# Chunks 0 and 1 of a delta-rule kernel rebuilt: four units side by side, 128-lane inversions, the pipeline from unit 4 on, and g @ w_out in step with the conversion of w_out

## The chip, the cores and the metric

The kernel runs on one core of a Trainium2 chip. The metric is the device time of one execution in microseconds (us). A profiled execution gives a span (first to last instruction) and a trace. The engines are PE (matrix multiplies; PEld is its weight load), DVE (vector), ACT (scalar), POOL (GpSimd) and SP, which issues most DMA transfers. Each engine works through its own instructions in order and meets the others by semaphores.

## The reference

Two stages. A delta rule runs over 768 positions for each of 4 x 8 heads with 48 columns, then a feed-forward block takes all 3072 rows:

```python
k_n = k / (np.linalg.norm(k, axis=-1, keepdims=True) + 1e-06)
for t in range(S):
    y[:, :, t] = np.einsum('bhd,bhde->bhe', q[:, :, t], state)
    v_old = np.einsum('bhde,bhd->bhe', state, kt)
    state = state + bt[:, :, :, None] * np.einsum('bhd,bhe->bhde', kt, vt - v_old)
# x = y as (3072, 384)
h = x @ w_in                              # 384 x 2048
g = h * (1.0 / (1.0 + np.exp(-1.702 * h)))
out = g @ w_out                           # 2048 x 384
```

The two weight matrices arrive in 64-bit floating point; the kernel converts them to 32 bits on the chip.

## The kernel before, in words

**Units.** The 768 positions are cut into 6 chunks of 128. A unit is one chunk c of one batch b with its 8 heads, `n = 4*c + b`, so there are 24 units; units 0 to 3 are chunk 0 and have no earlier state. Two units in a row make a pair, whose 256 rows go through the feed-forward block together.

**One unit.** `normalize` scales the keys. `prepare` transposes them (psT into kT), multiplies them with themselves (psG into G), and sends G through DRAM (Nd) so that the 32 x 32 blocks on its diagonal come back with one block a lane, in NT. A unit has 8 heads x 4 blocks = 32 blocks, so four units fill 128 lanes. `invert` (line 389) inverts these unit triangular blocks on DVE by row steps and then by products of halves, multiplies by beta into YS, and sends the result through DRAM (Yd) back as XB. It is a generator with 25 steps. For chunk 0 it runs once with 128 lanes; for each later pair of units once with 64 lanes. `Step.scores` (line 498) makes M, the masked product of keys and queries (psQ), with POOL's selection, and for c > 0 takes the state's share out of V. The substitution goes block by block: `solve` (psU, 16 records of PE, copied by ACT into US) and `below` (psR, subtracted from V by DVE in `rest`). `together` issues solves and belows of several units in turns. `outputs` multiplies M with US (psY) and copies the result to xT; `state` adds to ST. Some rows of xT go by six transfers from `last`.

**The feed-forward block.** `hidden` (line 623) computes ph = x @ w_in and ACT's Gelu into gT; `written` (line 644) computes po = g @ w_out and writes `out`. Both are generators that yield a cost in us. `take` draws from a queue of them.

**The weights.** `fetch` brings raw 64-bit parts into memory that w_out will fill later; `from_double` (line 166) converts a part with five operations on DVE, one of them followed by a Relu on ACT. w_in has 12 parts of 512 columns, w_out 16 of 384. A part can be fetched only when its place is free.

**The order.** Everything is issued from the end of the function (line 864 on): four units are prepared, `invert(0)` runs, three units are scored, and then step n runs for n = -1 to 24. A step works on three units at once: the last blocks of unit n-1 (A), the middle ones of n (B_) and the first of n+1 (D_). Steps up to 5 are `slot`, with six groups: each does some steps of the inversion, some parts of weights (WB = 1, 3, 5, 7, 8 per step) and feed-forward work for a share of 15.6 to 18.8 us; with nothing queued, `warm` runs small matmuls that only keep PE busy. Steps from 6 on are `woven`, with feed-forward work for 20.8 us in shares of a sixth. `pinned` (line 103) keeps an operation in the order in which it is written; a pinned operation is recorded in the trace at line 105, whatever its real line, so the groups are told apart by their tiles.

Of the kernel before, what the change touches and what calls it, by code (L numbers as in the profile page):

```python
# [18 lines left out]
def kernel(  # L19
# [33 lines left out]
    GR = 6  # L53
    NTH = HB * C
    FQ = 4
    GB = 4

    W0, W1, WB = 3, 1, (1, 3, 5, 7, 8)
    NA = W0

    NW, NA0, NY, NB0 = 80, 3, 48, 6
    XR = DP - D
    W = 6
    NS = C * C + C
    assert S % C == 0 and H == 8 and D <= DP and DM == H * D == KC * 128
    assert B == 4 and B * H * NB == 128 and FC == 4 * FQ
# [40 lines left out]
    in_order, now = [False], [0]  # L107

    class Engine:
# [5 lines left out]
        def __getattr__(self, name):  # L115
            op = getattr(self.engine, name)
            return pinned(op) if in_order[0] else op

    vec, act, pe = Engine(nc.vector), Engine(nc.scalar), Engine(nc.tensor)

    for i in range(B):
        nc.vector.memset(KN[i][:, :, D:DP], 0.0)
        load(i, ((KN, k),))

    bI = cpool.tile([128, NC, BS], F32, name="bI")
    betas = beta.rearrange("b h (c k j) -> (b h) c k j", k=NB, j=BS)
    for blk in range(NB):
        nc.scalar.dma_start(out=bI[blk::NB], in_=betas[:, :, blk, :])


    ident = cpool.tile([128, 128], F32, name="ident")
    make_identity(nc, ident)
    half = cpool.tile([128, H], F32, name="half")
    nc.gpsimd.memset(half, 0.5)

    nc.gpsimd.memset(YB, 0.0)
    nc.gpsimd.affine_select(
        out=YB, in_=YB, compare_op=ALU.not_equal, fill=1.0, base=0,
        pattern=[[1, BS], [-1, BS]], channel_multiplier=0,
    )  # L140


# [5 lines left out]
    def warm(n, after=None):  # L148

        ps = ps_moe.tile([128, 256], F32, tag="moe", name="ps_warm")  # L150
        if after is not None:
            after(ps[:, 0:1], 0.0)
        for _ in range(n):
            pe.matmul(ps, lhsT=ones[:, 0:128], rhs=ones, start=True, stop=True)  # L154

    warm(NW)
    table = cpool.tile([128, 1], F32, name="table")
    nc.scalar.activation(table, ident[:, 0:1], ACT.Copy)

    w_in = cpool.tile([128, KC, DFF], F32, name="w_in")  # L160
# [3 lines left out]
    nc.gpsimd.memset(low, -896.0 * (1 << 23))  # L164

    def from_double(dst, raw, n, alone):
# [5 lines left out]


        lo, hi = raw[:, :, 0], raw[:, :, 1]
        ts, stt = vec.tensor_scalar, vec.scalar_tensor_tensor
        if alone:
            ts, stt = pinned(ts), pinned(stt)
# [3 lines left out]

        ts(p, hi, 0x7FF * E1, None, op0=AND)
        if alone:
            ts(p, p, -896.0 * E1, 0.0, op0=ALU.add, op1=ALU.max)
            ts(p, p, 255.0 * E1, 8.0, op0=ALU.min, op1=ALU.mult)
        else:
            act.activation(p, p, ACT.Relu, scale=8.0, bias=low)
        yield
        t = wk.tile([128, n], I32, tag="P", name="tmp")
        f = t.bitcast(F32)  # L190
        ts(t, hi, E1 - 1, E1, op0=AND, op1=OR)
        stt(out=f, in0=lo.bitcast(U32), scalar=2.0**-32, in1=t, op0=ALU.mult, op1=ALU.add)
        stt(out=p, in0=hi, scalar=-(1 << 31), in1=p, op0=AND, op1=OR)
        stt(out=dst, in0=f, scalar=2.0**-20, in1=dst, op0=ALU.mult, op1=ALU.mult)
        yield

    N_IN = 512
    parts_in = KC * DFF // N_IN
    n_parts = parts_in + FC

    x_rows = [
        (ct * DP + o, (ct * NP + i) * D, m, step)
        for ct in range(2)
        for o, i, m, step in ((0, 0, D, D), (D, KC, XR, XR))
    ]

    stages, taken, made, begun = {}, {}, [], {}  # L210

    def stage(part):

        if part < parts_in:
            at = part % (2 * KC) * 2 * N_IN
            return at, at + 2 * N_IN
        f = part - parts_in
        if f >= FC - 2:
            return None
        depth = 2 if f < 2 or f >= 8 else 4  # L220
        if f >= 12:
            depth = 1
        at = FC * DM // (2 if f < 2 else 1) - (f % depth + 1) * 2 * DM
        return at, at + 2 * DM

    def together_with(part):

        return list(range(part, part + (KC if part < 3 * KC else 1)))

    def free(part):  # L230
        places = [s for p in together_with(part) if (s := stage(p)) is not None]
        return all(s[1] <= a or b <= s[0] for s in places for a, b in taken.values())

    def fetch(part, dma):

        if part < parts_in:
            j, f0 = part % KC, part // KC * N_IN
            parts = together_with(part)
            shape, src = (len(parts), N_IN), moe_w_in[:, f0 : f0 + N_IN]
            dst = w_in[:, j : j + len(parts), f0 : f0 + N_IN]  # L240
        else:
            parts = [part]
            shape, src = (1, DM), moe_w_out
            dst = target(part)
        if src.dtype != F32:
            if (s := stage(part)) is None:
                raw = wk.tile([128, *shape, 2], I32, tag="xT", name="raw", bufs=3)
            else:
                words = slice(s[0], stage(parts[-1])[1])
                raw = w_out.rearrange("p f d -> p (f d)")[:, words].bitcast(I32)  # L250
                raw = raw.rearrange("p (j n o) -> p j n o", j=shape[0], o=2)
            for i, p in enumerate(parts):
                stages[p] = raw[:, i]
                if s is not None:
                    taken[p] = stage(p)
            dst = raw.bitcast(src.dtype).rearrange("p j n o -> p j (n o)")
        if part < parts_in:
            for i in range(len(parts)):
                for p, r, m, step in x_rows:
                    dma(out=dst[p : p + m, i], in_=src[r + (j + i) * step : r + (j + i) * step + m])  # L260
        else:
            r = (part - parts_in) * 128
            dma(out=dst if src.dtype == F32 else dst[:, 0], in_=src[r : r + 128, :])
        return parts

    def target(part):
        if part < parts_in:
            j, f0 = part % KC, part // KC * N_IN
            return w_in[:, j, f0 : f0 + N_IN]
        return w_out[:, part - parts_in, :]  # L270

    def begin(part):

        if part not in begun:
            if part >= parts_in:
                a, b = (part - parts_in) * DM, (part - parts_in + 1) * DM
                if any(taken[p][0] < b and a < taken[p][1] for p in stages if p in taken):
                    return
            dst = target(part)
            begun[part] = from_double(dst, stages[part], dst.shape[-1], part < NA)  # L280
            next(begun[part])

    def convert(part):
        if part in stages:
            begin(part)
            if staged:
                begin(min(staged))
            stages.pop(part)
            next(begun.pop(part))

            made.append(part)
            while made and (len(made) > 1 or part < NA or part >= n_parts - 8):
                taken.pop(made.pop(0), None)


    ready = {}
    inverse = {}
# [431 lines left out]

    def slot(n, share):  # L730

# [197 lines left out]
```

## Time and profile before

| | us |
|---|---|
| median of three runs | 822.17 |
| all three | 822.04, 822.17, 824.47 |
| profiled execution | 821.86 |
| its span | 819.8 |
| PE busy in the span | 768.8 (94%) |
| DVE busy | 483.0 (59%) |
| ACT busy | 230.7 (28%) |
| POOL busy | 131.7 (16%) |
| mean granted clock of PE | 0.952 |

The profile's page cuts the span into 40 slices of 20.5 us; a digit is a busy share in tenths, and PEclk the clock granted to PE in tenths of full speed. A window line gives, for a stretch of the span, the busy time of each engine with its number of instructions. A timeline line gives start, duration, engine, line, operation, output<-inputs with shapes, and in brackets the idle time before and what ended it. In the trace each 32-bit matmul shows as two records; counts here are of records.

### The profile page before, as it was taken

The numbers are of one execution on the slowest core, as the hardware profiler recorded it, in microseconds if no ns is written. First come the engines' busy times: TensorE is split into PE (matmuls) and PEld (weight loads), VectorE is DVE, ScalarE is ACT, GpSimd is POOL, SyncE is SP. The second block draws the span as 40 slices with busy tenths as digits, with TensorE's granted clock in tenths as the row PEclk, the third lists the DMA queues.
The fourth block names the chain that finished last, engine by engine and source line by source line (L and its number), as shares of the span: only waits on it lengthen the run. The fifth ranks groups of instructions, "written<-read, shape, count | busy, mean of one in ns | idle before, by whom it ended". The sixth has DMA issues, their size and how long they took to land.

```text
span 819.8 us, 18780 instructions
## 1 busy us (share of the span) xinstructions
PE 768.8 (94%) x8100; PEld 577.4 (70%) x8100; DVE 483.0 (59%) x1037; ACT 230.7 (28%) x499; POOL 131.7 (16%) x138
## 2 busy tenths in 40 slices
PE   8429799889799999999999999999999999999998
PEld 7327688557676876867867867867768768677684
DVE  7797989787965675666667667666656730100000
ACT  2212543242232332322422322322322223212120
POOL 2013120322021222122123122212201000000000
PEclk9659889978979999999999999999999999999999
DMA  7986732721315123214204213213222020000000
GB/s 146 199 183 122 201 87 82 178 68 48 68 30 125 34 49 96 60 23 100 62 21 102 53 32 90 54 43 80 53 59 45 12 51 1 11 16 1 24 1 19
DMA packets 147698, 55.96 MB, mean 68 GB/s; under 512 B 114720, under 2 KB 143616, under 8 KB 147616
## 3 DMA queue, kind: packets, MB, share of 16 engines
q1 hardware_dynamic: 139872, 41.96, 24.0%
q0 software_dynamic: 2752, 10.62, 4.7%
q10 hardware_dynamic: 4992, 2.20, 1.0%
q8 instruction: 63, 1.03, 0.6%
q14 instruction: 19, 0.16, 0.1%
HBM read 33.13 MB, written 20.45 MB: 65 GB/s over the span
## 4 chain that ended last, share of the span: by engine, by line
PE 79%; DVE 6%; issue 6%; DMA 4%; SPq 2%; POOL 1%; ACT 1%; DVEq 0%; POOLq 0%; ACTq 0%
PE po L105 28%; PE ph L105 25%; PE psY L105 5%; PE psU L105 4%; PE psQ L105 3%; PE ps_warm L154 3%; PE ph L633 2%; PE psG L105 2%; PE psR L105 2%; DMA w_out<-in_moe_w_out_dram 2%; PE psT L105 1%; SPq L105 1%; DMA w_out<-in_moe_w_in_dram 1%; DVE tmp L105 1%; PE psG L362 1%
## 5 line engine op out<-in xcount | busy, mean ns | idle before, releaser
L105 PE MATMUL po<-w_out,gT 128*128 128x384 f32 x704 | 239.3, 490 | 0.0
L105 PE MATMUL ph<-xT,w_in 128*128 128x256 f32 x966 | 222.0, 384 | 0.3
L105 PEld LDWEIGHTS ph<-xT,w_in 128*128 128x128 f32 x966 | 180.3, 191 | 30.9 <-issue 2.3
L105 PEld LDWEIGHTS po<-w_out,gT 128*128 128x128 f32 x704 | 130.1, 190 | 82.6 <-issue 1.9
L105 DVE TENSOR_TENSOR V<-V,psR 64x384 f32<-64x384 f32 (+1 forms) x80 | 44.4, 556 | 194.8 <-PE psR L105 194.0
L105 DVE TENSOR_TENSOR P<-NT,YB 64x18 f32<-64x18 f32 (+25 forms) x171 | 82.3, 481 | 4.5
L105 ACT ACTIVATE gT<-ph 128x512 f32<-128x512 f32 x81 | 48.2, 595 | 115.9 <-PE ph L105 115.8
L105 DVE TENSOR_REDUCE YB<-P 64x6 f32<-64x18 f32 (+25 forms) x171 | 72.7, 425 | 5.5
L105 ACT COPY US<-psU 32x384 f32<-32x384 f32 x80 | 37.6, 470 | 131.9 <-PE psR L105 118.4
L528 POOL TENSOR_SCALAR_AFFINE_SELECT M<-M 128x1024 f32<-128x1024 f32 x24 | 29.8, 1240 | 226.6 <-DVE M L105 159.8
L105 PEld LDWEIGHTS psU<-V,XB 32*32 32x32 f32 x1280 | 45.9, 105 | 27.9 <-issue 20.5
L105 PE MATMUL psU<-V,XB 32*32 32x48 f32 x1280 | 54.3, 203 | 2.1 <-DVE V L105 2.1
L105 PE MATMUL psR<-US,G 32*32 32x48 f32 x1920 | 52.8, 203 | 0.0
L633 PE MATMUL ph<-xT,w_in 128*128 128x128 f32 (+1 forms) x282 | 47.0, 321 | 1.6 <-DMA xT<-last 1.6
L105 PEld LDWEIGHTS psR<-US,G 32*32 32x32 f32 x1920 | 44.6, 105 | 0.5 <-issue 0.5
L633 PEld LDWEIGHTS ph<-xT,w_in 128*128 128x128 f32 x282 | 40.3, 198 | 5.7 <-issue 2.4
L154 PE MATMUL ps_warm<-ident 128*128 128x256 bf16 x152 | 22.8, 318 | 16.7 <-DVE ps_warm L105 14.4
L90 POOL DMA_DIRECT2D KN<-in_k_dram x14 | 13.4, 955 | 153.1 <-PE psY L105 102.0
L308 POOL TENSOR_TENSOR rn<-ssq,half 128x8 f32<-128x8 f32 x17 | 36.9, 2169 | 2.9 <-DVE ssq L306 2.9
L105 ACT COPY o<-po 128x384 f32<-128x384 f32 x22 | 10.5, 479 | 77.7 <-PE po L105 55.8
L154 PEld LDWEIGHTS <-ident 128*128 128x128 bf16 x152 | 17.1, 114 | 21.0 <-issue 14.6
L105 DVE TENSOR_TENSOR P<-NT 64x256 f32<-64x256 f32 (+7 forms) x36 | 30.3, 841 | 0.3
(144 smaller groups left out, 871.0 us busy)
## 6 DMA issues: line engine op xcount, KB each, us to landing
Nd<-G SPq DMA_DIRECT2D x20, 512.0 KB, 3.5
w_out<-in_moe_w_out_dram POOLq DMA_DIRECT2D x14, 384.0 KB, 3.7
QP<-in_q_dram SPq DMA_DIRECT2D x24, 192.0 KB, 3.9
V<-in_v_dram SPq DMA_DIRECT2D x24, 192.0 KB, 3.0
out_dram<-o SPq DMA_DIRECT2D x24, 192.0 KB, 1.9
w_out<-in_moe_w_in_dram SPq DMA_DIRECT2D x18, 192.0 KB, 5.2
NT<-Nd SPq DMA_DIRECT2D x24, 128.0 KB, 2.6
Yd<-YS SPq DMA_DIRECT2D x24, 128.0 KB, 2.5
```

What stands on the lines that cost most here:

```text
L90: dma(out=dst[n % len(dst)][:, :, 0:D], in_=src[b, :, c * C : (c + 1) * C, :].rearrange("h p d -> p h d"),)
L105: return lambda *a, **kw: tc.keep_in_program_order(op(*a, **kw))
L154: pe.matmul(ps, lhsT=ones[:, 0:128], rhs=ones, start=True, stop=True)
L308: nc.gpsimd.tensor_tensor(rn, ssq, half, op=ALU.pow)
L362: pe.matmul(ps[h % 2][:, h // 2], lhsT=kT[r, h // 2, :], rhs=kT[r, h // 2, :], start=True, stop=True,)
L528: nc.gpsimd.affine_select(out=self.M, in_=self.M, compare_op=ALU.is_gt, fill=0.0, base=0, pattern=[[0, H], [1, 128]], channel_multiplier=-1,)
L633: pe.matmul(ph[:, u], lhsT=w_in[:, j, f * 128 : (f + 1) * 128], rhs=xT[:, j, t], start=(j == 0), stop=(j == KC - 1),)
```

## The change

Nothing changes in what is computed. In the new code:

- Keys of units 0 to 3 are normalized in one go, with the squares on ACT. A product of the transposed keys is made early (`turn`, `diagonal`), and only the 32 x 32 blocks are copied out and sent through DRAM as rows; the whole G of these units is made later (`gram`), while DVE inverts.
- All units 0 to 3 are scored before the substitution. Their POOL selections (`select`) wait on a `gate` that reads YS.
- The substitution of chunk 0 runs as units 0 and 1 side by side, then units 2 and 3 (`hops`), each ended by `put_out`.
- Units 4 to 7 are normalized and prepared during the second of these (`keys`), and inverted together with 128 lanes (`invert(1)`), beside the rest of `hidden` of pairs 0 and 1.
- Weights are converted in one sequence (`conversions`): w_in in 8 pieces of 3 x 256 columns, then w_out in 12 single and 2 double rows. `fill(n)` issues the next n operations of it. Each finished piece can trigger a fetch; all fetches go by SP, except half of the first two quarters of w_in, which go by POOL.
- `both_written` makes po of units 0 and 1 together and issues, ahead of each row f, as much of the conversion as that row needs and three operations more.
- `slot` is gone. `woven` runs from n = 3, with a share of 10.4 for n = 3 to 6 and 20.8 after.
- gT has 8 buffers instead of 4; some of them (`spare`) hold other tiles early. All vector, scalar and tensor operations are pinned now, as were those before step 2 and from step 6 on.

The core of the diff:

```diff
-    NW, NA0, NY, NB0 = 80, 3, 48, 6
+    GB = 8
     XR = DP - D
-    W = 6
+    NW, NA, NY, NU = 80, 3, 28, 4
+    NQ = DFF // 4
+    NPC = DFF // 8
     NS = C * C + C
...
+    def conversions():
+        whole = list(pieces())
+        def begin(i):
+            dst, raw, shape, name = whole[i]
+            ops = conversion(dst, places[name[1]] if raw is None else raw, shape)
+            next(ops)
+            return ops
+        after = begin(0)
+        yield
+        for i in range(len(whole)):
+            ops = after
+            next(ops)
+            yield
+            next(ops)
+            yield
+            if i + 1 < len(whole):
+                after = begin(i + 1)
+                yield
+            next(ops)
+            yield
+            next(ops)
+            done.add(whole[i][3])
+            fetches.pop(whole[i][3], lambda: None)()
+            yield
...
+    fetches = {
+        ("in", 1): lambda: fetch_in(2),
+        ("in", 3): lambda: fetch_in(3),
+        ("in", 5): lambda: fetch_out(3),
+        ("in", 7): lambda: (fetch_out(4), fetch_out(5), fetch_out(6), fetch_out(7)),
+        ("out", 4): lambda: fetch_out(13),
+        ("out", 6): lambda: fetch_out(12),
+    }
+    for new, old in ((8, 0), (9, 1), (10, 2), (11, 8), (14, 9), (15, 10)):
+        fetches[("out", old)] = lambda f=new: fetch_out(f)
+    converting = conversions()
+    def fill(n):
+        for _ in range(n):
+            next(converting, None)
...
+    def normalize_mixed(n):
+        K = KN[n % len(KN)][:, :, 0:D]
+        ksq = wk.tile([128, H, D], F32, tag="ksq", name="ksq", bufs=1)
+        act.activation(ksq, K, ACT.Square)
+        yield
+        ssq = wk.tile([128, H], F32, tag="ssq", name="ssq", bufs=4)
+        vec.tensor_reduce(ssq, ksq, axis=AX.X, op=ALU.add)
+        rn = wk.tile([128, H], F32, tag="rn", name="rn", bufs=4)
+        pool.tensor_tensor(rn, ssq, half, op=ALU.pow)
+        yield
+        vec.tensor_scalar(rn, rn, 1e-6, None, op0=ALU.add)
+        vec.reciprocal(rn, rn)
+        vec.tensor_tensor(K, K, rn.broadcast_to([128, H, D]), op=ALU.mult)
+        yield
...
+        for b in range(B):
+            act.activation(sq[:, b % 2], KN[b][:, :, 0:D], ACT.Square)
+            vec.tensor_reduce(s[:, b], sq[:, b % 2], axis=AX.X, op=add)
...
+        ready[n] = KN[n % len(KN)], kT, G
+        return G
...
+    def turn(n):
+        kTs[n] = wk.tile([128, NP, 128], F32, tag="kT", name="kT", bufs=6)
+        transposed(KN[n % len(KN)], kTs[n])
+    def prepare(n):
+        c, b = units[n]
+        turn(n)
+        yield 0.6
+        G = gram(n)
         Nd = dram.tile([H * NS], F32, tag="Nd", name="Nd", bufs=4)
-        dma = pinned(nc.scalar.dma_start) if c == 0 else nc.sync.dma_start
+        dma = sync if c < 3 else nc.sync.dma_start
...
+        dma(
...
+    def diagonal(b, D_):
+        kT = kTs[b]
+        ps = [ps_seq.tile([128, NP, 128], F32, tag="seq", name="psD") for _ in range(2)]
+        for h in range(H):
+            r = slice(h % 2 * 64, h % 2 * 64 + D)
+            pe.matmul(
+                ps[h % 2][:, h // 2], lhsT=kT[r, h // 2, :], rhs=kT[r, h // 2, :],
+                start=True, stop=True,
+            )
+        for e in range(2):
+            for blk in range(NB):
+                u = slice(blk * BS, (blk + 1) * BS)
+                copy = vec.tensor_copy if e == 0 or blk == 0 else act.copy
+                copy(D_[u, e::2, :], ps[e][u, :, u])
...
         YS = wk.tile([128, BS, BS], F32, tag="P", name="YS")[part]
         vec.tensor_tensor(YS, Y, bc, op=ALU.mult)
...
+        if c == 0:
+            gate = wk.tile([128, 1], F32, tag="gate", name="gate", bufs=1)
+            pool.tensor_copy(gate, YS[:, 0, 0:1])
+        dma = sync if c < 3 else nc.sync.dma_start
+        groups = [range(b0, b0 + nb)] if c > 0 else [range(HB), range(HB, B)]
+        back = {}
+        for bs in groups:
+            for b in bs:
+                back[b] = dram.tile([H * C, BS], F32, tag="Yd", name="Yd", bufs=4)
+                (beside if c == 0 and b >= HB else dma)(
+                    out=back[b].rearrange("(p j) i -> p j i", j=BS),
+                    in_=YS[(b - b0) * NB * H : (b - b0 + 1) * NB * H],
+                )
+            for b in bs:
+                XB = wk.tile([128, H, BS], F32, tag="XB", name="XB", bufs=4)
+                dma(out=XB, in_=back[b].rearrange("(h t) i -> t h i", h=H))
+                inverse[c * B + b] = XB
         yield 0.0
...
+        def select(self):
+            (pool if self.n < B else nc.gpsimd).affine_select(
...
+    def both_written(c, gT):
+        po = [ps_moe.tile([128, DM], F32, tag="moe", name="po") for _ in range(HB)]
+        for n, f in enumerate(order):
+            while ("out", f - f % 2 if 4 <= f < 8 else f) not in done:
+                fill(1)
+            fill(3)
+            for i in range(HB):
+                pe.matmul(
+                    po[i], lhsT=gT[f // FQ][:, f % FQ, i * C : (i + 1) * C], rhs=w_out[:, f, :],
+                    start=(n == 0), stop=(n == FC - 1),
+                )
+            if n < FC - 1:
...
-    def slot(n, share):
...
-                warm(NB0)
-        if n + 1 == len(WB) - 1:
-            run(weights(n_parts))
-        if n == W - 1:
-            next(new_step(n + 2).scored, None)
-        if n % HB == 0:
-            run(inverting)
-        follow(n)
...
+        if n % HB == 0 and n > B:
             h = (n - 1) // HB
-            if h == 0:
-                i = (n - 1) % HB
-                queue.append(hidden(xTs[h], gT0, slice(i * C, (i + 1) * C), 0.67))
-            if n % HB == 0:
-                gT = gT0 if h == 0 else []
-                if h > 0:
-                    queue.append(hidden(xTs[h], gT, slice(0, NTH), 1.3))
-                queue.append(written(*units[h * HB], gT))
-                xTs.pop(h)
+            gT = []
+            queue.append(hidden(xTs[h], gT, slice(0, NTH), 1.3))
+            queue.append(written(*units[h * HB], gT))
+            xTs.pop(h)
...
-        debt[0] += cost
+        debt[0] = debt[0] + cost if queue else 0.0
...
-        m, late = n + B + 1, n == W
+        m = n + B + 1
         K = normalize(m) if m < len(units) else iter(())
         P = prepare(m) if m < len(units) else iter(())
-        Q = prepare(m - 1) if late else iter(())
-        if n % HB == 1 and n + 1 + HB < len(units):
+        if n % HB == 1 and B < n and n + 1 + HB < len(units):
             inverting = invert(*units[n + 1 + HB], HB)
-        ahead = [8] * 3 if late else STEPS[:3] if n % HB == 1 else STEPS[3:]
+        ahead = STEPS[:3] if n % HB == 1 else STEPS[3:]
...
-        spend(share / 6)
-        next(Q, None)
-        spend(share / 6)
+        spend(share / 3)
...
+        sync(out=bI[blk::NB, 0], in_=betas[:, 0, blk, :])
...
+    fetch_in(0, other_queue)
...
+    warm(NW)
+    normalize_first()
+    Ds = spare("blocks").rearrange("p (b h j) -> p b h j", b=B, j=BS)
+    Nds = []
+    turn(0)
+    for b in range(B):
+        if b + 1 < B:
+            turn(b + 1)
+        diagonal(b, Ds[:, b])
+        Nd = dram.tile([H * C * BS], F32, tag="Nd", name="Nd", bufs=4)
+        sync(out=Nd.rearrange("(h p k) -> p h k", p=C, k=BS), in_=Ds[:, b])
+        Nds.append(Nd)
+    for b in range(B):
+        sync(
+            out=NT[b * NB * H : (b + 1) * NB * H].rearrange("d i k -> d (i k)"),
+            in_=Nds[b].rearrange("(d r) -> d r", r=BS * BS),
+        )
...
+    fetch_in(1, other_queue)
...
+    fill(6)
+    for b in range(B):
+        gram(b)
+        warm(NA)
+    pair = [new_step(n) for n in range(B)]
+    inverting = invert(0)
+    for n in range(B):
+        next(pair[n].scored)
+        warm(NA)
+        run(pair[n].scored)
+        warm(NA)
+        if n == 0:
+            ahead_of(inverting, 18)
+    run(inverting)
+    for s in pair:
+        s.select()
+    fill(5)
+    def hops(a, b):
+        yield [(a, 0)], []
+        for blk in range(NB - 1):
+            yield [(b, blk)], [(a, blk)]
+            yield [(a, blk + 1)], [(b, blk)]
+        yield [(b, NB - 1)], []
+    def put_out(s):
+        s.queries()
+        s.outputs(True)
+        steps.pop(s.n)
+    def keys():
+        def unit(n):
+            yield from normalize_mixed(n)
+            yield from prepare(n)
+        work = [unit(n) for n in range(B, 2 * B)]
+        for t in range(18):
+            for u in range(B):
+                s = t - 3 * u
+                if s >= 0 and s % 2 == 0:
+                    next(work[u], None)
+            yield
+        for w in work:
+            run(w)
+    path = hops(*pair[:2])
+    for i in range(2 * NB):
+        together(*next(path))
+        warm(NU)
+        fill(1)
+    for s in pair[:2]:
+        put_out(s)
+        fill(1)
+    load(7, ((KN, k),), sync)
+    load(8, ((KN, k),), sync)
+    for f in range(3):
+        fetch_out(f)
+    for n in range(B, B + 2):
+        load(n, ((QP, q),), sync)
+    ffn = []
+    def feed(n=1):
+        for _ in range(n):
+            while ffn and next(ffn[0], None) is None:
+                ffn.pop(0)
+    gTs = [], []
+    ffn.append(hidden(xTs[0], gTs[0], slice(0, NTH), 1.3))
+    path = hops(*pair[2:])
+    preparing = keys()
+    for i in range(2 * NB):
+        together(*next(path))
+        if i > 2:
+            feed()
+        fill(2)
+        ahead_of(preparing, 2 if i else 0)
+    for s in pair[2:]:
+        put_out(s)
+        feed()
+        fill(2)
+        ahead_of(preparing, 2)
+    ffn.append(hidden(xTs[1], gTs[1], slice(0, NTH), 1.3))
+    xTs.pop(0), xTs.pop(1)
+    load(B + 2, ((QP, q),), sync)
+    for n in range(B, B + 2):
+        load_values(n, sync)
+    while not ("in", 7) in done:
+        fill(1)
+    run(preparing)
+    inverting = invert(1)
+    first = new_step(B)
+    for i in range(25):
+        ahead_of(inverting, 1)
+        feed()
+        if i == 16:
+            next(first.scored)
+        if i == 18:
+            run(first.scored)
+    run(inverting)
+    while ffn:
+        feed()
+    fill(10)
+    queue = [both_written(0, gTs[0]), written(*units[HB], gTs[1])]
+    for n in range(B - 1, len(units) + 1):
+        woven(n, 20.8 if n > 6 else 10.4)
```

## The prediction

> **What bounds the kernel now.** I read the slices first, then the stretches of the span by engine, then single rows. The slices:
>
> ```profile
> PE   8429799889799999999999999999999999999998
> DVE  7797989787965675666667667666656730100000
> PEclk9659889978979999999999999999999999999999
> ```
>
> From slice 12 on (about 254 us) PE is full at full clock; before that DVE is the fuller engine and the clock dips. The same in four stretches (columns: length, then busy us of PE, weight load, DVE, ACT, POOL, then granted clock, DMA share, GB/s):
>
> ```profile
> 0.00:67.40 67.40, 38.44 (x298) 30.95 (x298) 57.26 (x140) 15.67 (x32) 13.10 (x32) 0.72 0.96 177
> 67.40:232.00 164.60, 146.20 (x1856) 113.58 (x1856) 138.01 (x305) 60.59 (x130) 32.31 (x39) 0.89 0.42 101
> 232.00:254.45 22.45, 22.45 (x260) 15.75 (x260) 20.05 (x33) 6.45 (x14) 4.41 (x4) 0.90 0.23 57
> 254.45:820.00 565.55, 561.68 (x5694) 417.13 (x5692) 267.65 (x562) 148.03 (x324) 81.87 (x64) 1.00 0.19 46
> ```
>
> 67.4 us is the first substitution (psU), 254.45 the end of unit 5's outputs (psY). After it PE bounds; before it DVE does 158 us of work in 187 us. So the change acts on the time until unit 5's outputs, and what follows it is counted in PE records. The waits of the first part, from the timeline (start, duration, instruction, idle before):
>
> ```profile
> 31.00 1.22 DVE L105 TENSOR_TENSOR NT<-NT,bI 128x1024 f32<-128x1024 f32 x1 [3.11 <-DMA NT<-Nd]
> ...
> 57.88 1.23 DVE L456 TENSOR_TENSOR YS<-YB,bI 128x1024 f32<-128x1024 f32 x1
> ...
> 67.44 0.86 PE L105 MATMUL psU<-V,XB 32*32 32x48 f32 x16
> ```
>
> The first inversion waits for its blocks until 31.0; YS ends it; the first solve follows 8 us later, behind 48 + 18 warm-up matmuls.
>
> **The tail, by records.** At the end PE runs one pair's ph (96 records) and po (64) back to back:
>
> ```profile
> 775.08 20.72 PE ph L105 x96
> 795.80 20.66 PE po L105 x64
> ```
>
> So a pair costs 41.38 us, a po record 0.323, a ph record 0.216. Before, 669 po and 960 ph records start after 254.45: 216.0 + 207.2 = 423.2 us. After the change, steps 3 to 6 spend 10.4 each on pairs 0 and 1 (41.6 in all, just their po: 41.3); at unit 5's outputs four of step 6's six shares are spent, so 3.5 is left, and ten pairs: 413.8 + 3.5 = 417.3. The attention work after that point is the same code. The rest is 565.4 (254.45 to 819.8) - 5.9 = **559.5 us**.
>
> **First solve: 67.4 to 60.** Squares go to ACT and one chain of small operations normalizes four units instead of two chains; but PE's 80 warm-ups end at 13.9 either way, so that earns nothing. Then PE needs 0.44 (psT x4) + 1.09 (psG x16) a unit; block copies cost DVE 5 x 0.28 a unit (row: last<-psY on DVE, 281 ns) and ACT 3 x 0.27 + 0.6, each within 1.53. Last copy 13.9 + 0.6 + 4 x 1.53 + 1.6 = 22.2. SP carries four beta loads more (one sixth of 24 KB each; before, all beta went by ACT) and six of the first quarter's twelve (0.42 each; POOL's six 0.54, ahead of memsets that nothing early needs): over by 10 us, before the blocks. Writing the blocks (a 128 KB transfer lands in 2.6 to 3.3) and reading them as whole rows (Yd: 2.2) gives NT at 28.0 instead of 31.0. The six conversion steps before it (4.6 us) lie in that wait, as 10 us of conversion did. The inversion took 26.9; two conversion operations in it (0.33 and 0.61 net) and two slow products beside POOL's selection (0.7, 0.2) are taken out: 25.0. YS ends at 54.2. The added gate holds POOL's four selections (1.1 to 1.3 each) behind YS: done by 60, first needed at 74. Yd to XB issue took 2.0, landing 3.3: 59.5; 28 warm-ups at 0.158 end before. First solve 60. Bounds: 57 if small blocks land as fast as Yd, 64 if as slowly as the 5.0 of the last G write.
>
> **Pairs 0/1: 60 to 78.5.** Eight calls: PE 0.88 (16 psU and 48 psR), then DVE 0.56, or 1.12 for block 0, plus 0.2 of signalling: 1.2 + 2 x 2.2 + 4 x 1.65 + 1.3 = 13.5; one more for Relu (some 1.0 on ACT) ahead of a US copy; two put_outs at 2.0. Warm-ups (4 x 0.145) and one conversion operation lie in the gaps. Before, the staggered start took 67.4 to 102 for two units.
>
> **Pairs 2/3: 78.5 to 112.** A conversion piece of 768 columns I scale from the rows of 384 and 512 columns (0.35, 0.42 and 0.55, 0.69): 2 x 0.56 + 3 x 0.97 = 4.0. A call has DVE 0.75 + 2 x 0.84 + 0.6 (norms of units 4 to 7: 4 x 1.47 spread) = 3.05, PE 0.88 + 1.3 + 0.7 = 2.9. So 2.2 + 2 x 2.9 + 5 x 3.05 + two put_outs at 3.3 = 30. **An added wait:** w_in's last quarter is asked for at 79.5, behind six xT transfers on SP (0.58 each) and needs 12 issues (0.42) and 5.1 to land: 92, wanted at 88.5. V's subtractions, norms and through V the next solves queue behind it on DVE: 3.5. Bounds 0 to 10 (issues of up to 1.5 are in the row).
>
> ACT's Square now alternates with the Gelu; the trace shows one table load of 1.28 at the first Gelu, and none for Relu and Copy after it, but has no Square. Up to two more loads, 0 to 2.6 us, on ACT, which is busy 2.3 of 3.05 a call: I take 0. The Trainium skill, "ScalarE: Activation LUTs", section "Table sets: the hidden batching unit", names relu, copy, identity and abs as in every set, not square, and its budget of about 2.7 us a switch would make it 5.3; an estimate that speaks against the change, and no run here shows it.
>
> **Inversion 1: 112 to 156.5.** One inversion of 128 lanes replaces two of 64 lanes: a product over 1024 columns is 1.22 in both, so 26 us of DVE go. It waits for unit 7: G copies 1.2, SP behind four w_out fetches, G's write 3.6, NT 2.6: starts 122; 25 + 1 (psQ subtractions) + 1.5 (their wait for PE) + 1.2 = 150.7. Beside it PE's 25 feeds take 32.4 + 2: to 147, so PE hides little more than DVE's wait. Ten conversion steps (5.5) follow, while XB lands: 156.5. Bounds 150 to 162.
>
> **Steps 3 and 4: 156.5 to 196.5.** By the order written out, 27 and 32 conversion operations at 0.47 (2.35 a piece: 0.35, 0.35 and 3 x 0.55), with subtractions, sums and norms 2 and 4: 18 + 19; PE's share is 13.3 and 16. Two gaps of 0.9, where three operations run ahead cover 1.4 of PE's 2.3; 1 for a fetch: 40. The nearest rows say the same: before, 14 conversions with two units' substitutions filled 144 to 182:
>
> ```profile
> 160.00:170.00 10.00, 9.25 (x52) 4.67 (x45) 8.97 (x20) 3.16 (x7) 5.08 (x6) 0.83 0.31 71
> 170.00:180.00 10.00, 7.62 (x99) 5.25 (x100) 8.07 (x24) 5.21 (x11) 3.40 (x3) 0.75 0.18 52
> 180.00:190.00 10.00, 10.00 (x103) 6.08 (x100) 5.76 (x15) 1.18 (x4) 0.97 (x1) 0.56 0.37 93
> ```
>
> These rows also show the clock falling to 0.56 where PE waits piecewise. For the whole start I add 4 (bounds 0 and 10). By the Trainium skill, "TensorE: Matmul & The Clock Gate", Part 1, "What's actually happening", the clock halves only after an idle window of about 3.4 us; no gap in my steps is that long, so by the rule the 4 is 0 and the end 798. The row differs: waits of under 2 us on PE lie in this stretch.
>
> **Step 5 and step 6 to unit 5's outputs: 40.** PE 10.4 + 8.5 (29.15 a step less 20.7) = 18.9, DVE 17 to 18 in line with it by sections: 21.5; NT of unit 9 comes 2.5 late; step 6 to the end of psY 16.
>
> **Sum.** 60 + 18.5 + 33.5 + 44.5 + 40 + 40 + 4 = 240.5, + 559.5 = 800.0 span; the profiled run took 821.86 for a span of 819.8, so 802.1; its time lies 0.3 under the median of 822.17.
>
> **Rivals.**
> - *DVE stays as full as it was* (0.845 until 254.45). My DVE work from first solve to that point is 135 (conversions 60, inversions 48, the rest 27): 160 us, unit 5's outputs at 220, end 781.5. For it: idle waits were short; against: NT of unit 7 and the feeds leave 10 us that nothing fills. Chance 0.12.
> - *The transfers come late*: quarter 3 at its 10, inversion 1 at 162, 4 more in step 5's NT and fetches: 6.5 + 5.5 + 4 = 16, end 818. The DMA share of 0.96 at the start speaks for it, 0.42 later against. 0.10.
> - *Slower: DVE and PE take turns in steps 3 and 4.* If three operations ahead cover nothing, PE's 29.3, less the 2.8 of gaps that I count already, stand behind DVE's 37: +26, 828. It decides once unit 5's outputs end 20 us after my 240.5. For it: po before waited for w_out (3.5 on weight loads) at low clock; against: those waits were 0.5 to 1.7 each. 0.16.
> - *It does not do what it says:* DVE only shifts the same waits, outputs at 256 to 261: 817.5 to 823, no change. 0.07.
>
> **Chances.** My case (786 to 814) 0.55. A measurement here tells about 0.3%, 2.5 us. Faster 0.55 + 0.12 + 0.10 = 0.77, same 0.07, slower 0.16. The range reaches to the first rival's time and leaves out what lies beyond it and most of the third: 781 to 824.
>
> **What would show it.** First solve by 60; NT at 28; DVE inverting at 122, idle ahead of it; one inversion of 128 lanes; psY of unit 5 ending near 240; then steps of 29.2 at full clock. Wrong if the clock in steps 3 to 6 is near 0.6, if conversions wait on transfers for over 10 us, or if steps from 7 on are not PE's.

## The result, and the profile after

Median after the change 823.73 us (20 runs, 818.19 to 831.47), before 824.63 (20 runs, 819.54 to 828.87): ratio 0.9989, interval 0.9965 to 1.0012. No change that can be measured. The forecast was 802.1. The profiled run took 823.91 for a span of 822.2 us.

The slices of the kernel after (tenths of each fortieth of the span):

```profile
PE   8678699777789999999999999999999999999998
DVE  5896671897679656675666566567665650110000
PEclk9686669889899999999999999999999999999999
```

PE is full from the thirteenth slice on, as it was before. DVE is no longer the fuller engine ahead of that; neither engine is full throughout. The chain of waits shows the last pair at the end of the run:

```profile
777.27 20.72 PE ph L102 x96
797.99 20.65 PE po L102 x64
```

That tail is the forecast's to 0.1 us a pair. So whatever was forecast and did not come is missing earlier. The stretches, cut where DVE starts or ends the stage (columns as before: length, busy us of PE, weight load, DVE, ACT, POOL, then granted clock, DMA share, GB/s):

```profile
0.00:61.90 61.90, 44.76 (x385) 35.22 (x386) 48.51 (x106) 23.80 (x54) 16.46 (x39) 0.81 0.81 135
61.90:84.60 22.70, 19.86 (x412) 15.65 (x413) 14.44 (x21) 6.69 (x14) 0.55 (x1) 0.70 0.38 81
84.60:128.00 43.40, 35.21 (x479) 27.64 (x477) 27.01 (x46) 18.80 (x36) 9.11 (x7) 0.69 0.63 137
128.00:146.15 18.15, 18.15 (x96) 15.73 (x95) 1.82 (x3) 5.21 (x10) 0.80 (x1) 1.00 0.62 164
146.15:174.10 27.95, 21.12 (x97) 17.67 (x96) 26.47 (x53) 6.54 (x14) 1.09 (x1) 0.88 0.21 38
174.10:228.00 53.90, 41.96 (x351) 24.85 (x353) 40.95 (x85) 17.56 (x33) 8.64 (x7) 0.84 0.43 111
228.00:263.00 35.00, 31.92 (x512) 21.52 (x507) 30.97 (x69) 10.82 (x27) 10.60 (x8) 1.00 0.24 60
263.00:822.00 559.00, 555.29 (x5672) 414.16 (x5672) 271.20 (x562) 148.67 (x325) 80.43 (x64) 1.00 0.20 47
```

The rows are: to the first solve, pairs 0/1, pairs 2/3, the wait for the second inversion's blocks, that inversion, conversions with steps 3 and 4, the rest to unit 5's outputs, the tail. In the fourth row DVE works 1.82 us of 18.15. The rows of DVE that mark the stages, from the timeline (start, duration, instruction, idle before it):

```profile
29.92 1.23 DVE L102 TENSOR_TENSOR NT<-NT,bI 128x1024 f32<-128x1024 f32 x1 [2.01 <-DMA QP<-in_q_dram]
...
55.18 1.23 DVE L102 TENSOR_TENSOR YS<-YB,bI 128x1024 f32<-128x1024 f32 x1
...
101.21 0.69 DVE L102 TENSOR_SCALAR w_in<-w_out 128x768 int32<-128x768 int32 x1 [6.14 <-DMA w_out<-in_moe_w_in_dram]
...
146.15 1.22 DVE L102 TENSOR_TENSOR NT<-NT,bI 128x1024 f32<-128x1024 f32 x1 [16.29 <-DMA NT<-Nd]
...
172.91 1.22 DVE L102 TENSOR_TENSOR YS<-YB,bI 128x1024 f32<-128x1024 f32 x1
```

Two waits for transfers stand out: 6.14 us for w_in's last quarter (the w_out buffer holds its raw form) and 16.29 for the blocks. SP's queue shows what the transfers were behind (start, time that the issues took, how many):

```profile
85.01 4.27 SPq L102 DMA_DIRECT2D xT<-last  x6
89.38 5.68 SPq L102 DMA_DIRECT2D w_out<-in_moe_w_in_dram  x12
...
130.14 3.68 SPq L102 DMA_DIRECT2D xT<-last  x6
133.87 2.00 SPq L102 DMA_DIRECT2D w_out<-in_moe_w_out_dram  x4
135.97 0.38 SPq L102 DMA_DIRECT2D Nd<-G  x1
143.58 0.32 SPq L102 DMA_DIRECT2D NT<-Nd  x1
```

Both times six xT transfers go first. The last unit's G is written only after them and after four fetches of w_out, and that write takes 7.6 us where the three before it took 3.2 to 4.3 (from the issue at 111.41, 119.14 and 125.92 to the issue of the read behind each). The waits of DVE and of PE from 173 to 262 us (total, times, longest):

```profile
DVE V L102 <- PE psR L102: 10.1, 4, 4.0
DVE V L102 <- PE psQ L102: 2.5, 4, 1.9
```

```profile
PE po L102 <- DVE w_out L102: 9.6, 5, 2.9
PE po L102 <- ACT w_out L102: 4.3, 1, 4.3
```

Here each waits for the other: DVE 12.6 us for PE, PE 13.9 us for a converted row of w_out.

### The profile page after: what moved, and what is told of

It is laid out like the page before. It is cut to its first block, busy times and chain, and to the rows that moved or that the text cites. A ratio compares the mean times of both kernels' runs of the same rounds, so it can differ in the third digit from the quotient of the medians.

```text
span 822.2 us, 18456 instructions
## 1 busy us (share of the span) xinstructions
PE 768.3 (93%) x7984; PEld 572.4 (70%) x7984; DVE 461.4 (56%) x939; ACT 238.1 (29%) x513; POOL 127.7 (16%) x126
## 3 DMA queue, kind: packets, MB, share of 16 engines
q8 instruction: 63, 1.03, 0.5%
## 4 chain that ended last, share of the span: by engine, by line
PE 76%; DVE 14%; DMA 4%; SPq 2%; ACT 1%; issue 1%; POOL 0%; DVEq 0%; POOLq 0%; ACTq 0%
PE po L102 29%; PE ph L102 26%; PE psY L102 6%; PE psU L102 5%; DVE P L102 4%; PE psQ L102 3%; DVE YB L102 3%; PE psG L102 3%; PE psT L102 2%; DMA w_out<-in_moe_w_in_dram 2%; PE psR L102 2%; SPq L102 2%; DVE NT L102 1%; DVE w_out L102 1%; DVE tmp L102 1%
## 5 line engine op out<-in xcount | busy, mean ns | idle before, releaser
L102 PE MATMUL po<-w_out,gT 128*128 128x384 f32 x768 | 271.3, 502 | 14.0 <-DVE w_out L102 9.6
L102 PE MATMUL ph<-xT,w_in 128*128 128x256 f32 x1152 | 268.1, 390 | 0.3
L102 PEld LDWEIGHTS ph<-xT,w_in 128*128 128x128 f32 x1152 | 218.7, 193 | 34.4 <-issue 1.5
L102 ACT ACTIVATE gT<-ph 128x512 f32<-128x512 f32 x96 | 56.4, 595 | 140.6 <-PE ph L102 140.5
L102 DVE TENSOR_TENSOR P<-NT,YB 64x8 f32<-64x8 f32 (+31 forms) x190 | 88.9, 468 | 5.4
L102 PEld LDWEIGHTS psU<-V,XB 32*32 32x32 f32 x1536 | 62.3, 110 | 40.7 <-issue 28.0
L102 DVE TENSOR_REDUCE YB<-P 64x4 f32<-64x8 f32 (+31 forms) x190 | 81.0, 426 | 6.5
L102 PE MATMUL psU<-V,XB 32*32 32x48 f32 x1536 | 73.6, 210 | 5.9 <-DVE V L102 5.2
L102 PE MATMUL psQ<-QS,kT 48*128 48x176 f32 (+1 forms) x384 | 35.9, 329 | 6.1 <-ACT QS L102 6.1
L102 PE MATMUL ps_warm<-ident 128*128 128x256 bf16 x176 | 29.9, 327 | 12.5 <-ACT G L102 7.4
L294 POOL TENSOR_TENSOR rn<-ssq,half 128x8 f32<-128x8 f32 x16 | 36.5, 2279 | 12.6 <-DVE ssq L102 12.6
L102 PEld LDWEIGHTS psQ<-QS,kT 48*128 48x128 f32 x384 | 29.6, 198 | 9.1 <-ACT QS L102 7.9
L102 DVE TENSOR_REDUCE NT<-P 64x64 f32<-64x1024 f32 (+7 forms) x40 | 32.6, 815 | 1.4
L102 PE MATMUL psG<-kT 48*128 48x128 f32 x384 | 32.0, 313 | 0.2
```

Of the source, the lines that this page charges most:

```text
L102: return lambda *a, **kw: tc.keep_in_program_order(op(*a, **kw))
L294: nc.gpsimd.tensor_tensor(rn, ssq, half, op=ALU.pow)
```

## The experiments

Five causes were put up. (1) The clock: pairs 0 to 3 ran at 0.69 to 0.70, and more warm-up matmuls would mend it. (2) The last quarter of w_in comes late, behind the xT transfers. (3) The last unit's blocks come late, through their place in the order and through the four fetches beside them. (4) DVE's conversions stand on the path in steps 3 and 4, and ten of them would have been free in the wait ahead of the inversion. (5) Three operations of look-ahead are too few. Against all five stands the rival that these waits cover one another, so that taking one away only brings up the next.

All ratios are to the kernel before, which ran beside each experiment. The kernel after did not: a gain "against the change" sets two such ratios against each other, and part of it can be another chip or another clock. Stage times are the starts of DVE's rows: ST of units 1, 3 and 5 (each unit's outputs), NT and YS of the second inversion. For the kernel after they are 84.2, 127.6, 263.0, 146.15 and 172.9.

### The clock: e1_more_warm and e2_no_warm

```
e1: hops of units 0/1:  warm(NU) -> warm(10)
    hops of units 2/3: + warm(30 if i == 3 else 6)   ahead of fill(2)
e2: hops of units 0/1: - warm(NU)
```

> The changed kernel with more warm-up matmuls in the substitution of chunk 0: 10 instead of 4 a call for units 0 and 1, and 6 a call (30 in the call where the weights come late) for units 2 and 3. Theory A, the granted clock (0.70 and 0.69 in these two stretches, where I had priced 4 us for the whole start) makes them long: the clock rises above 0.85, the stretch from the first solve to the last psY of unit 3 falls from 66.6 us to 55 to 59, the time by 7 to 10 us against the changed kernel. Theory B, the stretch is a chain of DVE, ACT and PE that wait for each other in turn, whatever the clock: the clock rises and the stretch stays at 66 or grows by what the added matmuls take (up to 8 us).

> The changed kernel without the four warm-up matmuls a call for units 0 and 1. Theory A: the clock there falls from 0.70 to about 0.55, the stretch of units 0 and 1 grows from 22.7 us by 3 to 5. Theory B: the stretch keeps its length within 1 us, the time stays.

e1: 820.0 us, 0.9938 (0.9897 to 0.9978), an interval that overlaps that of the change itself. e2: 818.47, 0.9927 (0.9897 to 0.9957). The warm-ups did lift the clock, as the stretches of e1 show:

```profile
61.00:81.40 20.40, 19.26 (x467) 16.11 (x468) 15.61 (x21) 7.28 (x15) 2.09 (x2) 1.00 0.44 100
81.40:121.30 39.90, 34.27 (x557) 27.49 (x555) 27.00 (x45) 18.83 (x36) 9.03 (x6) 0.96 0.67 146
```

From its first solve (61.6 in e1) to unit 1's outputs, pairs 0/1 took 19.8 us at 1.00, against 23.2 at 0.70. Pairs 2/3 took 40 at 0.96, against 43.4 at 0.69. Together that is 59.7 for 66.6, just short of theory A's 55 to 59. In the profiled run this gain stays (816.65 us); over ten runs, 814.81 to 831.19, only 3.7 us of the median are left, where 7 to 10 had been expected.

e2 met neither theory. Without the warm-ups the clock of pairs 0/1 did fall, to 0.60, but the stretch got shorter, 21.1 us for 23.2, where A had 3 to 5 more and B the same. So the warm-ups that were to help cost time there. The trace of the kernel after shows two groups of them, at full and at half clock:

```profile
61.82 0.61 PE L102 MATMUL ps_warm<-ident 128*128 128x256 bf16 x4
...
71.30 1.03 PE L102 MATMUL ps_warm<-ident 128*128 128x256 bf16 x4
```

Pairs 2/3, whose code e2 leaves alone, took 38.0 at 0.87. So a full clock goes with 3.4 us less in pairs 0/1 and up to 5 in pairs 2/3; that the clock is the cause is shown for neither.

### Last quarter by two queues: e5_quarter_two_queues

```
-  ("in", 3): lambda: fetch_in(3),
+  ("in", 3): lambda: fetch_in(3, other_queue),
```

> The changed kernel with half of the third fetch of w_in after its start (the last quarter) on POOL's queue instead of all on SP's. It was issued from 89.4 to 95.1 behind six xT transfers and DVE waited 6.1 us for it. If issue is what makes it late, the wait falls to 1 to 3 us, and the stretch of units 2 and 3 (43.4 us, 38 to 40 in the runs with other clocks) by 3 to 5, the time by 3 to 5. If the bytes are (1.6 MB for some 8 us), the wait stays at 5 to 6 and so does the time.

814.98 us, 0.988 (0.9839 to 0.9922). DVE's waits from 84 to 125 us now have, for the quarter:

```profile
DVE w_in L102 <- DMA w_out<-in_moe_w_in_dram: 1.6, 1, 1.6
```

The wait went from 6.1 to 1.6, and pairs 2/3 from 43.4 to 34.4 us; 33.5 had been forecast. Of the 9.0, 4.5 is the wait: for the most part issue made it late, not the bytes. The time fell by 8.8 us against the change's median, where 3 to 5 had been expected. The clock from 85 to 125 us was 0.82 here and 0.66 after the change, and unedited pairs 2/3 took 43.3 at 0.61 to 0.62 (e6, e7, e8), 39.0 at 0.74 (e4) and 38.0 at 0.87 (e2); so the other half goes with the clock. Its cause is open: e2 and e4 ran on one chip and e6, e7 and e8 on two others, so the chip is a rival, though e5 ran on the same chip as e6. Nothing was lost again behind it: NT to unit 5's outputs took 115.2 us, after the change 116.9.

### The blocks: e3_blocks_early and e7_fetch_late

```
e3, e7:
-  ("in", 7): lambda: (fetch_out(4), fetch_out(5), fetch_out(6), fetch_out(7)),
   ...
   run(preparing)
+  for f in range(4, 8):
+      fetch_out(f)
e3 only: for unit 3, ahead_of(preparing, 2) before put_out(s), not after it
```

> The changed kernel, with the last unit's G sent to DRAM before unit 3's outputs, and the four fetches of w_out rows 4 to 7 after it instead of ahead of it. Theory C: DVE's wait of 16.3 us ahead of the second inversion is SP's queue (six xT transfers and four fetches ahead of G's write, 4.7 us) and the fetches' bytes beside it (the write took 7.6 instead of 3.5): the inversion starts at 135 to 138 instead of 146.15, psQ's wait of 4.8 us for QS goes, and the time falls by 8 to 10 us. Rival: PE's feed-forward work beside the inversion is the bound (25 feeds of 1.3 us from 130 on), so the earlier inversion only waits later: the time falls by 0 to 3 us.

> The changed kernel in which only the four fetches of w_out rows 4 to 7 move, from ahead of the last G's write to behind its return; the order of the outputs stays. It splits what the early-blocks run joined. If the fetches' bytes beside the write made it slow (7.6 instead of 3.5 us), the wait before the second inversion falls by 5 to 6 us, of the 12 that both edits gave. If the place behind six xT transfers was what counted, it falls by 2 at most (the fetches' issue of 2.0).

e3: 815.24 us, 0.9893 (0.9857 to 0.9928). e7: 817.79, 0.9928 (0.9904 to 0.9953). DVE's row in e3:

```profile
132.21 1.23 DVE L102 TENSOR_TENSOR NT<-NT,bI 128x1024 f32<-128x1024 f32 x1 [4.14 <-DMA NT<-Nd]
```

and the write and read of the blocks on SP in e3 and in e7:

```profile
125.90 0.52 SPq L102 DMA_DIRECT2D Nd<-G  x1
129.68 0.32 SPq L102 DMA_DIRECT2D NT<-Nd  x1
```

```profile
131.07 3.70 SPq L102 DMA_DIRECT2D xT<-last  x6
134.81 0.58 SPq L102 DMA_DIRECT2D Nd<-G  x1
138.22 0.33 SPq L102 DMA_DIRECT2D NT<-Nd  x1
```

e7 takes away the fetches alone: the write takes 3.4 us, not 7.6, and DVE's wait goes from 16.29 to 10.08. e3 takes the write ahead of the xT transfers too: wait 4.14. From unit 3's outputs to the last YS row, after took 45.3 us, e7 39.1, e3 36.4. So the fetches cost 6.2 (the write is 4.2 shorter without them, and their own issue of 2.0 no longer stands ahead of it), the write's place 2.7 more. In e3 the inversion starts 14 us earlier and ends 10.6 earlier; it takes 30.1 from NT to YS, after 26.8, perhaps because PE's feeds beside it are less far along, which no run separates. The time fell by 8.5 us against the change's median, as theory C had it. Shown: the second inversion came late through its blocks.

### Conversions in the wait: e4_convert_first

```
   run(preparing)
+  fill(10)
   inverting = invert(1)
   ...
-  fill(10)
```

> The changed kernel with the ten conversion operations issued ahead of the second inversion instead of behind it, in DVE's idle 16 us. Theory D: po of units 0 and 1 and with it steps 3 and 4 go at DVE's pace, so the whole 5.5 us are saved: time down by 4 to 6 us. Rival: steps 3 and 4 are held by PE and its clock (0.84) or by turns between the engines; then the operations were hidden anyway and the time falls by less than 2 us.

814.54 us, 0.9879 (0.9837 to 0.9922). DVE's wait before NT fell from 16.29 to 10.64: the ten operations lie in it. From YS to unit 5's outputs after took 90.1 us, e4 86.0; four kernels unedited there (e1, e2, e5, e7) took 88.3 to 88.7, and e3, unedited there too, 91.5. So 2.3 to 4.1 of the 5.5 us of operations were on the path (5.5 by e3), between the two theories. The time fell by 9.2 us against the change's median. Of that, 4.4 us in pairs 2/3 lie ahead of the edit, at clock 0.74, and are not the edit's; why all four runs of e4 are that fast isn't shown.

### How much the conversions cost: e8_one_of_five and e6_six_ahead

```
e8: conversion(dst, raw, shape, short=False):
+      if short: five bare yields after the first operation, and return
       short is set for the pieces of w_out
e6: fill(3) -> fill(6) in both_written
```

e8 leaves out four of five DVE operations and the Relu of each w_out piece, so w_out holds only the exponents.

> The changed kernel, leaving out four of the five DVE operations (and the Relu) of every w_out piece, so that w_out holds only exponents; it is run for its time. From YS of the second inversion to unit 5's state sum the kernel takes 88 to 90 us. Theory E and D, w_out's conversion sets the pace of steps 3 and 4: 29 us of DVE go, and 12 to 18 us of that stretch. Rival, the units' own chain through three engines at 18.9 us of PE a step is what sets it: it falls by less than 8.

> The changed kernel with six conversion operations issued ahead of each row of w_out instead of three. In steps 3 to 6 DVE waits 12.6 us for PE (psR, psQ) and PE 9.6 for w_out. Theory E, they take turns and three operations ahead cover 1.4 us of PE's 2.3: DVE's waits fall to 5 to 7 us, the time by 4 to 6 us. Rival: the added operations stand ahead of the subtractions from V, so the units' own chain gets as much later: waits of PE for V grow by as much, the time moves by less than 2 us.

e8: 803.6 us, 0.9753 (0.9716 to 0.979). Its stretch from YS to unit 5's outputs, and PE's wait for w_out from 155 to 262 us:

```profile
173.45:246.94 73.49, 68.30 (x853) 44.03 (x854) 43.70 (x99) 19.97 (x48) 18.57 (x15) 0.95 0.42 110
```

```profile
PE po L102 <- DVE w_out L102: 0.5, 1, 0.5
```

After the change this stretch took 90.1 with DVE busy 73.1. DVE lost 29.4 us of work and the stretch 16.6; PE's waits for w_out went from 13.9 (9.6 and 4.3) to 0.5. So 16.6 of 29.4 stood on the path: not the whole, as full turn-taking would have it, but more than the 8 that the rival allowed. The Relus are gone too, so part of it can be ACT's (the 4.3).

e6: 822.08 us, 0.9954 (0.9919 to 0.9988); its interval overlaps that of the change itself, and 4 to 6 us had been expected. The stretch took 87.8 us. PE's wait for w_out on DVE fell from 9.6 to 3.3, but DVE's wait for psR rose from 10.1 to 11.0: with more look-ahead it is DVE that stands.

### Together: c1_three_edits, c2_four_edits, c4_keys_on_dve, c5_keys_and_warm

```
c1 = e3 + e4 + e5        c2 = c1 + e6
c4 = c2, and in woven: K = (normalize_mixed if n < 7 else normalize)(m)
c5 = c4 + warm(9) in hops of 0/1, warm(4 if i > 2 else 10) in hops of 2/3
```

> The changed kernel with three edits together: the last G ahead of the outputs and fetches, the ten conversion operations ahead of the second inversion, the last quarter on two queues. If the three causes are separate, gains add, less what the ten operations no longer find of idle time: against the changed kernel 8 + 2 + 3 = 11 to 15 us, a time of 809 to 813. If one clock state stands behind all three runs, no more than the best single edit: 814 to 816.

> The three edits together with six operations ahead. Theory E: 4 to 6 us below the kernel with the three edits. Rival: within 2 us of it.

> The four edits together, with the keys of units 8 to 11 scaled by ACT and DVE instead of POOL. PE's transposes waited 6.8 us for POOL's product in steps 3 to 6. If that wait is on the path, 3 to 6 us go and the time is 800 to 802. If DVE, which gets 0.56 a unit more, or V's chain ends last anyway, it stays within 2 us of the kernel with four edits (805.4).

> The same with more warm-up matmuls in both substitutions of chunk 0 (9 a call, then 10 and 4). Theory A: clock above 0.9 between 61 and 125 (0.50 and 0.83 with four edits), another 3 to 5 us less, and runs closer together. Theory B: within 2 us of the kernel before it, or slower by the matmuls.

c1: 809.85 us, 0.9819 (0.9783 to 0.9855). c2: 805.38, 0.9786 (0.9747 to 0.9824). c4: 805.44, 0.9781 (0.9749 to 0.9813). c5: 806.44, 0.9762 (0.9693 to 0.9831). c2's interval overlaps c1's, so whether six operations ahead add something there is not settled. c4 adds nothing to c2 that can be told, so PE's wait for POOL's product was not on the path. c5's runs lie from 798.33 to 812.33, further apart and not closer as theory A had it; more of its warm-ups can't be told. The slices of c2:

```profile
PE   8579889959899999999999999999999999999998
DVE  5897678797686666666566666656656630100000
PEclk9685599999999999999999999999999999999999
```

and its stretches from 61 us to unit 5's outputs:

```profile
61.00:86.00 25.00, 24.16 (x420) 18.89 (x421) 15.67 (x21) 7.37 (x15) 2.65 (x3) 0.52 0.42 83
86.00:122.50 36.50, 30.65 (x501) 24.50 (x500) 26.98 (x45) 19.76 (x38) 11.54 (x12) 0.81 0.72 168
122.50:129.00 6.50, 5.34 (x24) 4.36 (x24) 6.32 (x13) 2.07 (x5) 0.90 (x1) 1.00 0.67 156
129.00:160.60 31.60, 31.36 (x154) 26.88 (x154) 25.28 (x53) 9.71 (x20) 1.09 (x1) 1.00 0.41 115
160.60:224.00 63.40, 50.13 (x575) 31.34 (x576) 49.09 (x114) 19.96 (x42) 13.45 (x10) 0.95 0.36 92
224.00:243.60 19.60, 18.92 (x282) 12.70 (x282) 17.57 (x32) 6.83 (x17) 6.22 (x5) 1.00 0.31 75
```

The wait ahead of the second inversion is now 6.5 us with DVE busy in 6.32 of it. Unit 5's outputs end at 243.6, against 263.0 after the change; 240.5 had been forecast. c1 is 13.9 us under the change's median, more than any single edit of its three, so one wait doesn't merely bring up the next. But the gains don't add by their times: e3, e4 and e5 alone are 8.5, 9.2 and 8.8 us under that median, 26.4 together. By the stages that the edits act on, 8.9 (blocks), 2.3 to 4.1 (conversions) and 4.5 (quarter) make 15.7 to 17.5, near c1's gain. c2 is 18.4 us under the median, or 16.7 by the ratios. c2 and c4 are faster than the kernel before by 2.1 and 2.2%, with intervals that reach from 1.8 to 2.5%.

## Why the prediction was wrong, step by step

The sum was 240.5 to unit 5's outputs and 559.5 after them. Measured: 263.0 and 559.2. So 22.5 us are missing, all before unit 5's outputs:

| Step | Forecast | Measured | Off |
|---|---|---|---|
| First solve | 60 | 61.0 | +1.0 |
| Pairs 0/1 | 18.5 | 23.2 | +4.7 |
| Pairs 2/3 | 33.5 | 43.4 | +9.9 |
| Wait for NT of unit 7's blocks | 10 | 18.5 | +8.5 |
| Inversion to the end of YS | 28.7 | 28.0 | -0.7 |
| Ten conversions, steps 3 and 4, to the last conversion's end (224.4) | 45.8 | 50.3 | +4.5 |
| To unit 5's outputs | 40 | 38.6 | -1.4 |
| Clock, as a term of its own | 4 | in the rows above | -4 |

- **Right:** the tail by records, the first solve (NT at 29.9 for 28; YS ending 56.4 for 54.2), one inversion for two, the steps after the conversions. DVE's work up to unit 5's outputs fell from 215.3 us to 190.2 by the stretches, by 25.1 where 26 had been counted.
- **Square beside Gelu: right at 0.** The groups of the kernel after hold two table loads on ACT, 1283 ns each, the start's and the first Gelu's, and no third, though Square and Gelu alternate. By the Trainium skill, "ScalarE: Activation LUTs", section "Table sets: the hidden batching unit", with its 2.7 us a switch, 5.3 had been the estimate; the measurement decides against that reading.
- **Failed: the wait for NT.** The step named the four fetches ahead of G's write, and then priced the write at the 3.6 of an undisturbed row. It took 7.6 beside them, and six xT transfers (3.68 us of issues) stood ahead of it on SP as well, which the step put at nothing. e7 and e3 put 6.2 and 2.7 us on the two, of which the step's sum leaves 2.6 for the fetches' issue. This is the largest cause that is shown, 8.5 of the 22.5.
- **Mis-sized: the last quarter in pairs 2/3.** 3.5 forecast, 6.1 measured, within its bounds of 0 to 10. The six xT issues took 4.27 us where six at 0.58 make 3.5, and the twelve of the quarter 5.68 where twelve at 0.42 make 5.0: 1.4 of the 2.6 us is slower issue. The trace of before had six xT issues that took 4.59, at 118.27. Another 1.1 is the step's own adding: 79.5 + 3.5 + 5.0 + 5.1 is 93.1, not 92.
- **Failed: warm-ups in the gaps of pairs 0/1.** The step put a call's four warm-ups (4 x 0.145) into gaps of PE. They fit only while the clock is full (61 to 69 us). From 73 to 81 us PE's records fill 8.00 of 8.00 us at a clock of 0.50, and the four take 1.03 us a call instead of 0.61, on the path. Without them (e2) 2.1 of the row's 4.7 go, at a still lower clock.
- **Mis-sized: the clock.** 4 us for the whole start; 3.4 us in pairs 0/1 and up to 5 in pairs 2/3 go with it by the runs at other clocks. The 3.4 and the warm-ups' 2.1 overlap, and the rest of both rows isn't told apart. The Trainium skill, "TensorE: Matmul & The Clock Gate", Part 1, "What's actually happening", made it 0 by its idle window of about 3.4 us; the longest gap of PE that the trace shows in pairs 0 to 3 is 3.1 (in steps 3 and 4 it is 4.35), so in pairs 0 to 3 the measurement differs. In c2's first row above PE is busy 24.16 of 25.00 us and the granted clock is 0.52. The prediction read its row of 0.56 as a clock that falls where PE waits piecewise, but PE is busy for all 10.00 us of that row. So busy records are not enough for the full clock here, and why isn't settled.
- **Mis-sized: the gaps of steps 3 and 4.** Between 174.1 and 224.4 DVE works 41.0 us, where the forecast had 43, and stands idle for 9.4, where it had 2.8; 8.2 of them wait for PE (psR 6.1, psQ 2.1). The 18 for the first of the two steps doesn't follow from its terms (27 x 0.47 + 2 is 14.7), but DVE's total was not too low by it.
- **The rival "DVE stays as full as it was"** fell: from 61.9 us to unit 5's outputs DVE is busy for 0.70 of the time, where it had 0.845.
- **The rival "DVE and PE take turns"** was worth 26 us, and its point of decision (20 us over 240.5) was passed, but not by its mechanism: the stretch is 4.5 longer than forecast, not 26. e8 shows that conversions stand on the path for 16.6 of 29.4 us, so DVE is the pace there only in part; the forecast had it for nearly the whole.
- **The rival "the transfers come late"** at 818 named the right place. It had the inversion's end at 162; it was 174.1.
- **The rival "it does not do what it says"** (817.5 to 823, outputs at 256 to 261, chance 0.07) comes nearest in time, and by luck: it had DVE shift the old waits, and what the runs show are two new ones and a low clock.
- **The signs.** DVE's start at 122 and unit 5's end near 240 failed, as they should. But none of the three signs of being wrong came: the clock in steps 3 to 6 was 0.84 and 1.00, the longest wait of a conversion for a transfer 6.14 us, and the tail is PE's. None of them watched the steps that failed.

So the change does what it was counted for: one inversion fewer and the first solve 6.4 us earlier. It loses as much again to two waits that it brings in, through the order on SP's queue, to warm-ups on the path, and to a low clock in pairs 0 to 3. That c2 ends unit 5's outputs within 3.1 us of the forecast does not prove the sum. Its rows differ both ways: pairs 0/1 took 24.1 for 18.5 and the inversion 32.8 for 28.7, while the wait was 6.5 for 10 and held the ten conversions, which the forecast had behind the inversion.

## What to carry to other kernels

When a step is moved, write down the issuing queue's order around it, transfer by transfer, and price a write that others wait for by a row with the same traffic beside it, not by a quiet one. Here a large saving on one engine that did not move the time was found again as idle time of that engine with a DMA for its releaser, and moving first the other transfers and then the write itself split it. Check what could be done in such a gap: ten conversions after a wait of 16 us were worth 2 to 4 us ahead of it. And work that is only to keep an engine busy has to be priced at the low clock too: there it can be the path.

## What the runs showed of the hardware that was not expected

- The same kernel scatters by its clock. Over 20 runs of the kernel after, span and mean granted clock go together at about -504 us per unit of clock (correlation -0.78): 816.5 us at 0.949 and 829.8 at 0.932 are two of them. So 13 us lie between runs, more than e3, e4 or e5 gives, and a stage time of one profile has to be read with its clock. Which of the two follows from the other isn't shown.
- A G write that took 3.2 to 4.3 us took 7.6 beside four w_out fetches, and 3.4 again without them (e7).
- Four conversion operations of 768 columns beside POOL's selections (56.6 to 62.4 us in the kernel after) took 1.21, 1.57, 1.57 and 1.72 us; the same forms later take 0.96, 0.69, 0.96 and 0.96.
